# Attention in single-bank tiles: float32 projections in quarter tiles, steps by halves of the heads, squares of the prologue summed by TensorE

## The chip, the cores and the metric

One Trainium2 chip, one of its cores. The metric is device time in microseconds; the median of three runs is given where there are several. Engines: TensorE (PE; its weight loads are PEld), VectorE (DVE), ScalarE (ACT), GpSimd (POOL) and SyncE (SP), which here only issues transfers.

## What is computed

Attention with random features for 4 batches of 8 heads, 576 tokens, head width 64 and 128 features, and behind it two feed-forward layers, the first with one expert per token out of 8.

```python
def phi(x):                                   # x = q or k, scaled by 64 ** -0.25
    proj = np.einsum('bhsd,md->bhsm', x, omega)
    h = proj - np.sum(x * x, axis=-1, keepdims=True) / 2.0
    return np.exp(h - np.max(h, axis=-1, keepdims=True)) / np.sqrt(m)
kv = np.einsum('bhsm,bhsd->bhmd', k_p, v)
num = np.einsum('bhsm,bhmd->bhsd', q_p, kv)
den = np.einsum('bhsm,bhm->bhs', q_p, np.sum(k_p, axis=2))[..., None] + 1e-06
x = (num / den)                               # then by tokens: 2304 x 512
expert_idx = np.argmax(x @ w_gate, axis=1)    # one expert: relu(x @ w1) @ w2, times its probability
out = np.maximum(x @ w_in, 0.0) ** 2 @ w_out
```

All of it is float32.

## The kernel before, in words

The 2304 tokens are 18 tiles of 128; a batch of 576 tokens is four and a half tiles, so tiles 4 and 13 belong to two batches (`pieces`). The order of every instruction is written out by hand: each engine works through its own queue in the order of the program, and SP's and POOL's queues issue the transfers.

For each K tile and each Q tile the kernel loads the tile twice, with the features down the partitions (`load`, L164) and with the tokens down the partitions (`load_rows`, L184). The first copy is split into a high part (`colsplit`, ScalarE, L223) and a rest (`colrest`, L234, POOL, or VectorE for the first seven K tiles). `proj` (L238) multiplies both with the two parts of omega: 12 matmuls of 256 columns into two PSUM banks of four heads each. The second copy is squared on POOL (`squares`, L201) and summed on VectorE (`sums`, L208). `most` (L262) takes the maxima of both banks on VectorE, `shift` (L268, L270) makes the bias of eight heads, and `expo` (L282) runs eight exponentials of 128 columns on ScalarE.

A K tile then goes into `kv_part` (L297): 16 float32 matmuls in half tiles (128 rows, 64 columns) that add the tile to its batch's product, in banks `w0` and `w1` until the batch ends. `kv_close` copies it out; `kvg_turn` (L320) and `kvg` (L329) append its product with the gate weights. A Q tile goes through `t_step` (L348, eight transposes into the pair of banks `t`; half is copied out by ScalarE, half by VectorE in `t_rest`), `n_step` (L369, 16 float32 matmuls in half tiles of 73 columns, then denominator, reciprocal and division for all heads on VectorE, L377 to L381) and `x_step` (L391, four transposes, one copy to `xT` on ScalarE and one store of `xT` to device memory from SP).

`attention` (L453) has a prologue for K tiles 0 to 4, 13 steps s that each take K tile s+5 and Q tile s, and steps 13 to 17 that take Q tiles alone. A Q tile is projected in step s, exponentiated in step s+1, transposed and multiplied in step s+2, and its x transposed in step s+3. The last two tiles' transposes and numerators stand behind the loop in `main_path`, between the first layers of the first two expert steps. The function `beside` puts the loads and splits of the first batch's expert weights into the steps from 8 on; the expert is chosen by `gating` and `counting` of the first batch in steps 7 and 8. Behind the attention the expert steps run, a batch's half and an eighth of the hidden width at a time, with the other loads and splits at steps that `plan` lists.

PSUM has eight banks: three `pj`, one `x`, the pair `t` and `w0`, `w1`.

Of the kernel before, what the change touches and what calls it, by code (L numbers as in the profile page):

```python
# [15 lines left out]
P = 128  # L16
B, H, S, D = 4, 8, 576, 64
M = 128
# [71 lines left out]
class Kern:  # L90
# [30 lines left out]
    def bank(self, tag, name):  # L121
        return self.ps.tile([P, 512], F32, tag=tag, name=name, bufs=3 if tag == "pj" else 1)

    def banks(self, name):
        return self.ps.tile([P, 2, 512], F32, tag="t", name=name, bufs=1)

    def setup_attn(self):
# [9 lines left out]
        self.hl, self.three = {}, {}  # L137
# [6 lines left out]
        self.womh = self.qpool.tile([P, 2 * M], F32R, name="womh")  # L144
        self.woml = self.qpool.tile([P, 2 * M], F32R, name="woml")
        nc.vector.tensor_copy(self.womh, w)
        nc.vector.tensor_tensor(self.woml, w, self.womh.bitcast(F32), ALU.subtract)
# [14 lines left out]
    def load(self, tag, t):  # L162

        if t >= NT:  # L164
            return
        pool = self.kpool if tag == "kp" else self.qpool
        x = pool.tile([P, DM], F32, tag=tag + "c", name=f"{tag}c{t}", bufs=3 if tag == "kp" else 2)
        self.nc.sync.dma_start(out=x, in_=self.a["kk" if tag == "kp" else "qq"][t, :, 0, :])
        self.cols[tag, t] = x

    def load_v(self, t):
        if t >= NT:
            return
        if len(pieces(t)) == 2:
            self.vin[t] = self.halves
            for i in range(2):
                rows = slice(i * 64, (i + 1) * 64)
                self.nc.sync.dma_start(out=self.halves[i][rows], in_=self.a["vv"][t, rows])
            return
        v = self.kpool.tile([P, H, VW], F32, tag="vin", name=f"vin{t}", bufs=5)  # L180
        self.vin[t] = [v]
        self.nc.sync.dma_start(out=v, in_=self.a["vv"][t])

    def load_rows(self, tag, t):  # L184
        if t >= NT:
            return
        if tag == "kp" and t < 8:
            if t % 2 == 0:
                self.pair = self.stage(f"kpr{t}")
            x = self.pair[:, t % 2 * DM : (t % 2 + 1) * DM]  # L190
        else:
            pool = self.kpool if tag == "kp" else self.qpool
            x = pool.tile([P, DM], F32, tag=tag + "r", name=f"{tag}r{t}", bufs=2)
# [3 lines left out]
    def squares(self, tag, t):  # L197
# [3 lines left out]
        self.nc.gpsimd.tensor_tensor(x, x, x, ALU.mult)  # L201

    def sums(self, tag, t):
        if t >= NT:
            return
        sq = self.rows.pop((tag, t))
        ssq = self.qpool.tile([P, H, 1], F32, tag="ssq", name=f"ssq_{tag}{t}", bufs=3)
        self.nc.vector.tensor_reduce(ssq, sq.rearrange("p (h d) -> p h d", h=H), axis=AX.X, op=ALU.add)  # L208
        three = self.three[tag, t] = self.qpool.tile([P, H, 3], F32, tag="three", name=f"three_{tag}{t}", bufs=5)
        self.nc.gpsimd.tensor_scalar(three[:, :, 1:2], ssq, -0.5 * SCALE * SCALE, None, op0=ALU.mult)  # L210
        if tag == "qp" or t > 5:
            self.load_rows(tag, t + 2)
        if tag == "qp" and t < 13 or tag == "kp" and t > 4:
            self.squares(tag, t + 1)

    def colsplit(self, tag, t):
        if t >= NT:
            return
        nc = self.nc
        pool = self.kpool if tag == "kp" else self.qpool  # L220
        x = self.cols.pop((tag, t))
        hi = pool.tile([P, DM], F32R, tag=tag + "h", name=f"{tag}h{t}", bufs=2)
        nc.scalar.copy(hi, x)  # L223
        self.hl[tag, t] = x, hi

    def colrest(self, tag, t):
        if t >= NT:
            return
        nc = self.nc
        pool = self.kpool if tag == "kp" else self.qpool  # L230
        x, hi = self.hl[tag, t]
        lo = pool.tile([P, DM], F32R, tag=tag + "l", name=f"{tag}l{t}", bufs=2)
        eng = nc.vector if tag == "kp" and t < 7 else nc.gpsimd
        eng.tensor_tensor(lo, x, hi.bitcast(F32), ALU.subtract)  # L234
        self.hl[tag, t] = hi, lo
        self.load(tag, t + (3 if tag == "kp" else 2))

    def proj(self, tag, t):  # L238

        nc = self.nc  # L240
        xh, xl = self.hl.pop((tag, t))
        if tag == "kp" and t in (2, 5):
            ps = [self.bank("pj", f"pj_{tag}{t}"), self.bank("x", f"pj_{tag}{t}_1")]
        elif tag == "kp" and t in (1, 4, 6):
            both = self.banks(f"pj_{tag}{t}")
            ps = [both[:, i, :] for i in range(2)]
        else:
            ps = [self.bank("pj", f"pj_{tag}{t}_{i}") for i in range(2)]
        self.pj[tag, t] = ps
        for c in range(H // 2):  # L250
            out = ps[c // 2][:, c % 2 * 2 * M : (c % 2 + 1) * 2 * M]
            s = slice(c * P, (c + 1) * P)
            nc.tensor.matmul(out, xh[:, s], self.womh, start=(c % 2 == 0), stop=False, skip_group_check=True)
            nc.tensor.matmul(out, xh[:, s], self.woml, start=False, stop=False, skip_group_check=True)
            nc.tensor.matmul(out, xl[:, s], self.womh, start=False, stop=(c % 2 == 1), skip_group_check=True)

    def most(self, tag, t):

        three = self.three[tag, t]
        for i, ps in enumerate(self.pj[tag, t]):  # L260
            out = three[:, 4 * i : 4 * i + 4, 0:1]
            self.nc.vector.tensor_reduce(out, ps.rearrange("p (h m) -> p h m", h=4), axis=AX.X, op=ALU.max)  # L262

    def shift(self, tag, t):

        nc = self.nc
        three = self.three.pop((tag, t))
        nc.vector.tensor_reduce(three[:, :, 2:3], three[:, :, 0:2], axis=AX.X, op=ALU.add, negate=True)  # L268
        bias = self.qpool.tile([P, H], F32, tag="bias", name=f"bias_{tag}{t}", bufs=3)
        nc.vector.tensor_reduce(bias, three[:, :, 1:3], axis=AX.X, op=ALU.add)  # L270
        self.bias[tag, t] = bias

    def expo(self, tag, t):

        nc = self.nc
        ps, bias = self.pj.pop((tag, t)), self.bias.pop((tag, t))
        if tag == "kp":
            y = self.kp[t] = self.kpool.tile([P, H, M], F32, tag=tag, name=f"kp{t}", bufs=3)
        else:
            y = self.qp[t] = self.qpool.tile([P, H, M], F32, tag=tag, name=f"qp{t}", bufs=2)  # L280
        for h in range(H):
            nc.scalar.activation(y[:, h, :], ps[h // 4][:, h % 4 * M : (h % 4 + 1) * M], AF.Exp, bias=bias[:, h : h + 1])  # L282
# [4 lines left out]
    def kv_part(self, b, t, i):  # L287
# [4 lines left out]
        if t == tiles[0]:  # L292
            self.kv_ps[b, i] = self.bank(f"w{i}", f"kv_ps{b}_{i}")
        part = [bb for bb, lo, hi in pieces(t)].index(b)
        for j in range(4):
            for a in range(0, M, 64):
# [4 lines left out]
                    start=(t == tiles[0] and j == 0),  # L301
# [4 lines left out]
    def kv_close(self, b):  # L306
        kv = self.kv[b] = self.qpool.tile([P, 2, 4, XW], F32, tag="kv", name=f"kv{b}", bufs=2)
        self.kvn = self.qpool.tile([P, 2, 4, D], F32, tag="kvn", name=f"kvn{b}", bufs=1)
        for i in range(2):
            ps = self.kv_ps[b, i][:, : 4 * VW].rearrange("p (h w) -> p h w", w=VW)  # L310
            self.nc.vector.tensor_copy(kv[:, i, :, 0:VW], ps)
            self.nc.scalar.copy(self.kvn[:, i], kv[:, i, :, 0:D])

    def kvg_turn(self, b):
# [3 lines left out]
        ps = self.bank("x", f"kvT_ps{b}")  # L318
# [5 lines left out]
    def kvg(self, b):  # L324

        nc = self.nc
        ps = self.bank("x", f"kvg_ps{b}")
# [10 lines left out]
    def t_step(self, t, apart=False):  # L338
        nc = self.nc
        qp = self.qp.pop(t)  # L340
        out = self.qpool.tile([P, 2, 512], F32, tag="qpT", name=f"qpT{t}", bufs=2)
        if apart:
            ps = [self.bank(f"w{i}", f"t_ps{t}_{i}") for i in range(2)]
        else:
            both = self.banks(f"t_ps{t}")
            ps = [both[:, i, :] for i in range(2)]
        for h in range(H):
            nc.tensor.transpose(ps[h // 4][:, h % 4 * P : (h % 4 + 1) * P], qp[:, h, :], self.ident)  # L348
        nc.scalar.copy(out[:, 1, :], ps[1])
        self.qpT[t] = out, ps[0]  # L350

    def t_rest(self, t):
        out, ps = self.qpT[t]
        self.nc.vector.tensor_copy(out[:, 0, :], ps)
        self.qpT[t] = out

    def n_step(self, t):

        nc = self.nc
        qpT = self.qpT.pop(t)  # L360
        x = self.qpool.tile([P, 2, 4, D], F32, tag="xr", name=f"xr{t}", bufs=2)
        lg = self.qpool.tile([P, 2, 4, E], F32, tag="lgh", name=f"lgh{t}", bufs=2)
        rd = self.qpool.tile([P, 2, 4, 1], F32, tag="rd", name=f"rd{t}", bufs=2)
        ps = self.banks(f"n_ps{t}")
        for i in range(2):
            for j in range(4):
                for a in range(0, P, 64):
                    b = next(b for b, lo, hi in pieces(t) if lo <= a < hi)
                    nc.tensor.matmul(  # L369
                        ps[a : a + 64, i, j * XW : (j + 1) * XW],  # L370
                        qpT[:, i, j * P + a : j * P + a + 64],
                        self.kv[b][:, i, j],
                        start=True,
                        stop=True,
                    )
        pv = ps[:, :, : 4 * XW].rearrange("p a (h w) -> p a h w", h=4)
        nc.vector.tensor_scalar(rd, pv[:, :, :, D : D + 1], 1e-6 * M, None, op0=ALU.add)  # L377
        nc.vector.reciprocal(rd, rd)
        nc.vector.tensor_tensor(x, pv[:, :, :, 0:D], rd.to_broadcast([P, 2, 4, D]), ALU.mult)
# [934 lines left out]
```

## Time and profile before

| what | us |
|---|---|
| median of 3 runs | 743.47 (743.17 to 747.55) |
| the profiled execution, device time | 748.41 |
| its span, first to last instruction | 746.9 |
| attention, to the last tile's first transpose | 153.14 |

The profile is of one execution. Its times count from the first instruction. A timeline row gives start, length, engine, line, operation, output and inputs, shape and count; rows of one kind that follow each other are merged. An engine's row says in brackets how long the engine stood idle before it and what ended that.

### The profile page before, as it was taken

What the parts mean: (1) busy time and instruction counts of PE and PEld (TensorE: products, weight loads), DVE (VectorE), ACT (ScalarE), POOL (GpSimd) and SP (SyncE); (2) the same over time, 40 slices, a digit from 0 to 9 for tenths busy, and PEclk for the clock granted to TensorE, in tenths of its full rate; (3) what the DMA queues carried; (4) which work ended last, traced back from release to release, by engine and by line L of the source; (5) the groups of instructions that cost most, each with busy time, mean ns of one, the idle gap of its engine ahead of it and who ended that gap; (6) DMA issues with size and microseconds to landing.
All of it is one profiled execution on the core that took longest, in us unless ns stands there. A gap on an engine that the chain in (4) does not pass through costs nothing.

```text
span 746.9 us, 16913 instructions
## 1 busy us (share of the span) xinstructions
PE 721.7 (97%) x6408; PEld 702.8 (94%) x6408; DVE 560.9 (75%) x1199; ACT 421.0 (56%) x1025; POOL 225.4 (30%) x298
## 2 busy tenths in 40 slices
PE   8899999999999999999999999999999989999996
PEld 7788888898999998999999999999999979999996
DVE  6888987877777667855665769687855898888892
ACT  5888888854455445544664546555742465554551
POOL 4756678811000014263731124144221200000000
PEclk9999999999999999999999999999999999999999
DMA  8757665735767677622043456466766374444421
GB/s 286 250 173 211 210 208 157 220 114 175 243 219 249 227 224 266 210 93 64 29 144 133 171 175 233 179 214 216 266 235 210 115 238 137 140 141 138 134 94 32
DMA packets 74536, 133.86 MB, mean 179 GB/s; under 512 B 8496, under 2 KB 36544, under 8 KB 74448
## 3 DMA queue, kind: packets, MB, share of 16 engines
q1 hardware_dynamic: 62192, 89.76, 36.7%
q0 software_dynamic: 12256, 42.95, 17.7%
q8 instruction: 52, 0.85, 0.5%
q14 instruction: 36, 0.29, 0.1%
HBM read 92.36 MB, written 40.32 MB: 178 GB/s over the span
## 4 chain that ended last, share of the span: by engine, by line
PE 68%; DVE 11%; DMA 8%; ACT 5%; issue 4%; POOL 1%; SPq 0%; ACTq 0%; DVEq 0%; POOLq 0%
PE y L1079 6%; PE y L1077 6%; PE y L1078 6%; PE X L963 4%; PE X L964 4%; PE X L965 4%; PE h L769 4%; PE h L768 4%; PE h L770 4%; PE y L797 3%; PE y L798 3%; PE y L796 3%; PE Z L963 2%; PE Z L964 2%; DMA xT<-wscr 2%
## 5 line engine op out<-in xcount | busy, mean ns | idle before, releaser
L780 ACT ACTIVATE hh<-h 128x288 fp32r<-128x288 f32 x64 | 26.3, 411 | 83.1 <-PE h L770 82.6
L939 ACT COPY xT<-X 128x288 f32<-128x288 f32 x96 | 37.0, 399 | 39.7 <-PE X L965 39.1
L1033 ACT CAST hc<-xT 128x384 fp32r<-128x384 f32 (+1 forms) x76 | 39.2, 563 | 29.7 <-DVE xT L63 18.3
L628 POOL DMA_DIRECT2D we<-we x32 | 17.8, 556 | 112.8 <-DVE hl L781 53.3
L282 ACT ACTIVATE kp<-pj_kp,bias_kp 128x128 f32<-128x128 f32 x144 | 39.3, 397 | 18.1 <-DVE bias_kp L270 15.0
L781 DVE SCALAR_TENSOR_TENSOR hl<-h,hh 128x288 fp32r<-128x288 f32 x64 | 29.0, 453 | 22.9 <-ACT hh L780 22.4
L1079 PE MATMUL y<-wB,hc 128*128 128x256 f32 x152 | 43.4, 286 | 0.6 <-DVE hc L1035 0.6
L1077 PE MATMUL y<-wB,hc 128*128 128x256 f32 x152 | 43.1, 283 | 0.0
L1078 PE MATMUL y<-wB,hc 128*128 128x256 f32 x152 | 43.0, 283 | 0.0
L1035 DVE TENSOR_TENSOR hc<-xT,hc 128x384 fp32r<-128x384 f32 (+1 forms) x76 | 42.2, 618 | 0.0
L282 ACT ACTIVATE qp<-pj_qp,bias_qp 128x128 f32<-128x128 f32 x144 | 39.5, 405 | 2.9 <-DVE rd L377 2.0
L769 PE MATMUL h<-xl,wA 128*128 128x288 f32 x128 | 38.2, 298 | 1.9 <-DVE xl L757 1.9
L732 DVE TENSOR_SCALAR narrow<-narrow 128x512 f32<-128x512 f32 x32 | 15.7, 490 | 31.8 <-ACT narrow L731 31.6
L942 DVE SCALAR_TENSOR_TENSOR xT<-xT 128x288 f32<-128x288 f32 (+1 forms) x64 | 39.3, 650 | 0.0
L797 PE MATMUL y<-hl,wA 128*128 128x288 f32 x128 | 38.0, 297 | 1.3 <-DVE hl L781 1.3
L768 PE MATMUL h<-xh,wA 128*128 128x288 f32 x128 | 38.3, 300 | 0.3 <-ACT xh L755 0.3
L963 PE MATMUL X<-wA,w 128*128 128x288 f32 x128 | 38.0, 297 | 0.5 <-ACT xT L805 0.5
L797 PE MATMUL y<-hl,wB 128*128 128x288 f32 x128 | 37.8, 295 | 0.3 <-DVE hl L781 0.3
L796 PE MATMUL y<-hh,wA 128*128 128x288 f32 x128 | 37.9, 296 | 0.0
L769 PE MATMUL h<-xl,wB 128*128 128x288 f32 x128 | 37.9, 296 | 0.0
L963 PE MATMUL X<-wB,w 128*128 128x288 f32 x128 | 37.9, 296 | 0.0
L768 PE MATMUL h<-xh,wB 128*128 128x288 f32 x128 | 37.8, 296 | 0.0
(247 smaller groups left out, 3001.5 us busy)
## 6 DMA issues: line engine op xcount, KB each, us to landing
hscr<-xT SPq DMA_DIRECT2D x32, 576.0 KB, 3.8
we<-we POOLq DMA_DIRECT2D x32, 512.0 KB, 5.5
xT<-hscr SPq DMA_DIRECT2D x64, 256.0 KB, 4.5
xT<-wscr POOLq DMA_DIRECT2D x48, 256.0 KB, 4.1
wd<-wf SPq DMA_DIRECT2D x22, 512.0 KB, 5.4
wscr<-narrow SPq DMA_DIRECT2D x22, 256.0 KB, 3.0
wd<-wf POOLq DMA_DIRECT2D x10, 512.0 KB, 4.3
kpc<-kk SPq DMA_DIRECT2D x18, 256.0 KB, 3.8
```

The costliest lines, as they stand in the source:

```text
L282: nc.scalar.activation(y[:, h, :], ps[h // 4][:, h % 4 * M : (h % 4 + 1) * M], AF.Exp, bias=bias[:, h : h + 1])
L768: nc.tensor.matmul(ps, w1, xh, start=(c == 0), stop=False)
L769: nc.tensor.matmul(ps, w1, xl, start=False, stop=False)
L796: nc.tensor.matmul(out, w1, hh, start=(f == 0), stop=False)
L797: nc.tensor.matmul(out, w1, hl, start=False, stop=False)
L942: nc.vector.scalar_tensor_tensor(v, v, 0.0, v, op0=ALU.max, op1=ALU.mult)
L963: nc.tensor.matmul(ps, w1, xh[:, r, c], start=(start and c == 0), stop=False, skip_group_check=True)
L964: nc.tensor.matmul(ps, w1, xl[:, r, c], start=False, stop=False, skip_group_check=True)
L1035: nc.vector.tensor_tensor(hc[q].at(1, a, b), raw[:, q, a + 1 : b + 1], hc[q].at(0, a, b).bitcast(F32), ALU.subtract)
L1077: nc.tensor.matmul(ps, h1, w1, start=first, stop=False, skip_group_check=True)
L1078: nc.tensor.matmul(ps, h1, w2, start=False, stop=False, skip_group_check=True)
L1079: nc.tensor.matmul(ps, h2, w1, start=False, stop=last, skip_group_check=True)
```

## The change

The split into high part and rest goes. `proj` multiplies the float32 tile itself, one head at a time, in quarter tiles (64 rows, 64 columns, 128 moving columns): 16 matmuls, where the even heads go to one bank and the odd heads to the other. Every step function works by halves, each with a single-bank tile, and the banks are named `k0`, `k1` (K projections), `q0`, `q1` (Q projections), `t0`, `t1` (transposes, numerators, x, counts) and `w0`, `w1` (kv, kvg).

For K tiles 0 to 4 the rows are not loaded: POOL squares the feature tile and TensorE sums the squares with four float32 matmuls against two columns that hold -0.5 times the squared scale, into free columns of the kv banks. For the other tiles POOL also adds the two halves of the squares, so that VectorE sums 32 columns a head instead of 64.

The numerators' division is cut in two, the order within a step is new, a Q tile is exponentiated in the step in which it is projected and transposed in the next, the gate products of a tile are kept and summed later, and the first batch's choice of an expert is spread over the steps 6 to 9 (`aside`). The loop of Q tiles runs to step 18. x is stored per batch (`x_store`) at the expert steps 2, 6, 10 and 14 instead of per tile.

The core of the diff:

```diff
     def sums(self, tag, t):
-        self.nc.vector.tensor_reduce(ssq, sq.rearrange("p (h d) -> p h d", h=H), axis=AX.X, op=ALU.add)
+        self.nc.vector.tensor_reduce(ssq, sq, axis=AX.X, op=ALU.add)
...
+    def colsums(self, t):
+        sq = self.sqc.pop(t)
+        w = t % 2
+        if t < 2:
+            self.kv_ps[0, w] = self.bank(f"w{w}", f"kv_ps0_{w}")
+        ps = self.kv_ps[0, w][:, 4 * VW + t * H : 4 * VW + (t + 1) * H]
+        for c in range(KC):
+            self.nc.tensor.matmul(ps[:, 2 * c : 2 * c + 2], sq[:, c * P : (c + 1) * P], self.half, start=(t < 2 and c == 0), stop=True, skip_group_check=True)
...
+    def proj(self, tag, t, banks):
+        x = self.cols.pop((tag, t))
+        ps = self.pj[tag, t] = [self.bank(f"{banks}{i}", f"pj_{tag}{t}_{i}") for i in range(2)]
+        for c in range(H // 2):
+            for a in range(0, P, 64):
+                for r in range(2):
+                    rows = slice(r * D, (r + 1) * D)
+                    nc.tensor.matmul(
+                        ps[r][a : a + 64, c * M : (c + 1) * M],
+                        x[rows, c * P + a : c * P + a + 64],
+                        self.wom[rows, r * M : (r + 1) * M],
...
         for s in range(13):
             k = s + 5
+            b = {1: 0, 5: 1, 10: 2}.get(s)
+            if s > 0:
+                self.proj("qp", s, "q")
+            if b is not None:
+                self.kvg_turn(b)
+            self.x_step(s - 2)
+            self.n_lg(s - 2, 1)
+            both("qp", s)
+            self.shift("qp", s)
+            if s > 0:
+                self.sums("kp", k)
+            self.shifted("qp", s)
+            if s > 0:
+                self.proj("kp", k, "k")
+            self.sums("qp", s + 1)
+            self.expo("qp", s, 0)
+            for i, c in ((1, nc.vector.tensor_copy), (0, nc.vector.tensor_copy if s < 3 else nc.scalar.copy)):
+                self.t_step(s - 1, i, "t", c)
+            self.t_copy(s - 1, 1)
+            self.t_copy(s - 1, 0)
+            if b is not None:
+                self.kvg(b)
+            self.expo("qp", s, 1)
+            self.most("kp", k, 0)
+            if b is None:
+                kv(s + 4)
+            self.most("kp", k, 1)
+            self.shift("kp", k)
...
+            self.load_v(k + 1)
+            self.n_step(s - 1, 0)
+            self.n_step(s - 1, 1)
+            self.n_den(s - 1, 0)
+            if s > 0:
+                self.shifted("kp", k)
+            self.n_rec(s - 1, 0)
+            self.n_den(s - 1, 1)
+            self.n_out(s - 1, 0)
+            self.n_lg(s - 1, 0)
+            self.n_rec(s - 1, 1)
+            expo("kp", k)
+            self.n_out(s - 1, 1)
...
+        for b in range(B):
+            at(2 + 4 * b, self.x_store, b)
```

## Rows read from the trace of the kernel before

**Rows 1.** The page's first part: busy time and share of TensorE.
```profile
PE 721.7 (97%) x6408; PEld 702.8 (94%) x6408; DVE 560.9 (75%) x1199; ACT 421.0 (56%) x1025; POOL 225.4 (30%) x298
```

**Rows 2.** Stretches of 10 us: busy time of each engine, clock, DMA share, GB/s.
```profile
60.00:70.00 10.00, 9.98 (x150) 9.09 (x148) 9.28 (x22) 9.21 (x29) 6.82 (x9) 1.00 0.71 221
...
200.00:210.00 10.00, 10.00 (x78) 10.00 (x77) 8.56 (x17) 5.24 (x11) 0.77 (x2) 1.00 0.67 230
```

**Rows 3.** Timeline of TensorE: transposes of Q tiles 0, 3, 12 and 17.
```profile
35.10 1.85 PE L348 MATMUL t_ps<-ident,qp 128*128 128x128 f32 x8 [2.23 <-ACT kp L282]
...
59.76 1.03 PE L348 MATMUL t_ps<-ident,qp 128*128 128x128 f32 x8
...
129.63 1.09 PE L348 MATMUL t_ps<-ident,qp 128*128 128x128 f32 x8
...
153.14 1.09 PE L348 MATMUL t_ps<-ident,qp 128*128 128x128 f32 x8
```

**Rows 4.** Timeline of TensorE in step 6.
```profile
66.85 1.04 PE L348 MATMUL t_ps<-ident,qp 128*128 128x128 f32 x8
67.73 0.60 PE L320 MATMUL kvT_ps<-ident,kvn 128*128 128x128 f32 x4
68.26 1.15 PE L297 MATMUL kv_ps<-vin,kp 128*64 128x65 f32 x32
69.34 1.07 PE L329 MATMUL kvg_ps<-wg,kvT 128*128 128x16 f32 x8
70.25 0.36 PE L253 MATMUL pj_kp<-womh,kph 128*128 128x256 f32 x1
...
71.59 0.28 PE L255 MATMUL pj_kp<-womh,kpl 128*128 128x256 f32 x1
71.79 1.25 PE L369 MATMUL n_ps<-kv,qpT 128*64 128x73 f32 x32
72.97 0.66 PE L391 MATMUL x_ps<-ident,xr 128*128 128x128 f32 x4
73.39 0.37 PE L253 MATMUL pj_qp<-womh,qph 128*128 128x256 f32 x1
```

**Rows 5.** Timeline of VectorE in step 6.
```profile
68.14 0.68 DVE L208 TENSOR_REDUCE ssq_kp<-kpr 128x8 f32<-128x512 f32 x1
...
72.70 0.17 DVE L268 TENSOR_REDUCE three_kp<-three_kp 128x8 f32<-128x16 f32 x1
```

**Rows 6.** Timeline of ScalarE in step 6.
```profile
68.94 2.19 ACT L282 ACTIVATE qp<-pj_qp,bias_qp 128x128 f32<-128x128 f32 x8
70.95 0.69 ACT L223 CAST kph<-kpc 128x512 fp32r<-128x512 f32 x1
73.17 1.66 ACT L282 ACTIVATE kp<-pj_kp,bias_kp 128x128 f32<-128x128 f32 x6 [1.54 <-DVE bias_kp L270]
```

**Rows 7.** Groups of 0 to 300 us: count, busy us, mean ns, idle before.
```profile
L262 DVE TENSOR_REDUCE three_qp<-pj_qp 128x4 f32<-128x512 f32 x36 | 23.9, 685 | 1.5 <-PE pj_qp L255 0.7
...
L234 POOL TENSOR_TENSOR qpl<-qpc,qph 128x512 fp32r<-128x512 f32 x18 | 23.0, 1279 | 27.7 <-ACT qph L223 27.6
```

**Rows 8.** Short stretches of the numerators: matmuls, then weight loads, in flight.
```profile
71.79:71.80 0.01, 0.01 (x2) 0.01 (x2) 1.00 1.05 410
...
71.91:71.92 0.01, 0.01 (x4) 0.01 (x6) 1.00 4.01 819
```

**Rows 9.** Timeline of the prologue, all engines.
```profile
4.11 0.62 ACT L223 CAST kph<-kpc 128x512 fp32r<-128x512 f32 x1 [1.86 <-DMA kpc<-kk]
...
5.77 0.41 PE L255 MATMUL pj_kp<-womh,kpl 128*128 128x256 f32 x1
5.98 0.41 PE L253 MATMUL pj_kp<-womh,kph 128*128 128x256 f32 x1
...
11.77 2.17 ACT L282 ACTIVATE kp<-pj_kp,bias_kp 128x128 f32<-128x128 f32 x8 [3.22 <-DVE bias_kp L270]
...
30.24 2.23 ACT L282 ACTIVATE qp<-pj_qp,bias_qp 128x128 f32<-128x128 f32 x8
```

More of the change, by code (lines that the diff above doesn't have):

```diff
@@ L227, in colrest, with most @@
+    def most(self, tag, t, r):
         if t >= NT:
             return
-        nc = self.nc
[L230 to L282, printed above, removed]
+        three = self.trio(tag, t).rearrange("p (c r) k -> p r c k", r=2)
@@ L291, in kv_part @@
         tiles = self.tiles_of(b)
-        if t == tiles[0]:
+        if t == tiles[0] and (b, i) not in self.kv_ps:
             self.kv_ps[b, i] = self.bank(f"w{i}", f"kv_ps{b}_{i}")
@@ L300, in kv_part @@
                     self.vin[t][part][:, 4 * i + j, :],
[L301 removed]
+                    start=(t == tiles[0] and j == 0 and b > 0),
                     stop=(t == tiles[-1]),
@@ L352, in t_rest @@
[L352 to L379, printed above, removed]
-        nc.vector.tensor_tensor(lg, pv[:, :, :, VW:], rd.to_broadcast([P, 2, 4, E]), ALU.mult)
-        nc.vector.tensor_reduce(self.lg[:, t, :], lg.rearrange("p a h e -> p e (a h)"), axis=AX.X, op=ALU.add)
-        self.xr[t] = x.rearrange("p a h d -> p (a h d)")
@@ new lines, in t_step, with t_copy @@
+    def t_step(self, t, i, tag, copy):
+        if not 0 <= t < NT:
+            return
+        qp = self.qp[t]
+        ps = self.bank(f"{tag}{i}", f"t_ps{t}_{i}")
+        for j in range(4):
+            self.nc.tensor.transpose(ps[:, j * P : (j + 1) * P], qp[:, 4 * i + j, :], self.ident)
+        out = self.qpT[t, i] = self.qpool.tile([P, 512], F32, tag=f"qpT{i}", name=f"qpT{t}_{i}", bufs=2)
+        self.tps[t, i] = lambda: copy(out, ps)
+    def t_copy(self, t, i):
+        if 0 <= t < NT:
+            self.tps.pop((t, i))()
@@ new lines, in n_step @@
+    def n_step(self, t, i):
+        nc = self.nc
+        if not 0 <= t < NT:
+            return
+        qpT = self.qpT.pop((t, i))
+        ps = self.bank(f"t{i}", f"n_ps{t}_{i}")
+        for j in range(4):
+            for a in range(0, P, 64):
+                b = next(b for b, lo, hi in pieces(t) if lo <= a < hi)
+                nc.tensor.matmul(
+                    ps[a : a + 64, j * XW : (j + 1) * XW],
+                    qpT[:, j * P + a : j * P + a + 64],
+                    self.kv[b][:, i, j],
+                    start=True,
+                    stop=True,
+                    skip_group_check=True,
+                )
+        self.nps[t, i] = ps[:, : 4 * XW].rearrange("p (h w) -> p h w", h=4)
```

415 lines of the change are left out of this document (241 added, 174 removed).

## The prediction

> **What bounds the kernel now.** I read the page's engine shares first: TensorE counts as busy for 97% of the span [rows 1], but that is a mean over two different stages. The stretches of 10 us tell them apart [rows 2]: from 200 us on TensorE alone is full (10.00 of 10, VectorE 8.56, ScalarE 5.24), while at 60 to 70 us TensorE, VectorE and ScalarE are all at 9 to 10 of 10. The change touches only this first stage, which ends with the transposes of the last tile at 153.14 us [rows 3]. What comes behind is bound by TensorE and is untouched, apart from one set of stores. So the gain is how much earlier that last transpose starts.
>
> Inside the stage I read one step on each engine. On TensorE the step runs from one `t_ps` to the next; its pieces in order are transposes 0.88, turn of kv 0.53, kv 1.08, kvg 0.9, K projection 1.54, numerators 1.18, x 0.42 (I use 0.5), Q projection 1.4 without its wait for a bank [rows 4]. I take pieces from start to start, since busy times of single matmuls overlap: the first and the last of the 12 matmuls of the K projection lie 1.34 apart, 0.12 a matmul, so 12 are about 1.4. On VectorE a sum of squares over 512 columns takes 0.68 and a small reduction of the bias 0.17 [rows 5]. On ScalarE eight exponentials take 2.01 (68.94 to 70.95) and a split copy 0.69, and ScalarE stood 1.54 us waiting for VectorE's bias [rows 6]. A maximum over 512 columns costs VectorE 0.685, and POOL's subtraction for the low part 1.28 [rows 7]. No engine is the bound by itself: the step with no kvg from tile 3 (59.76) to tile 4 (66.85) is 7.1 us, where TensorE's pieces sum to about 6.5. From the first `t_ps` at 35.10 to that of tile 12 at 129.63 are 12 steps, 7.88 each on average; from there to tile 17 at 153.14 are 23.5 us [rows 3].
>
> **The change part by part.** (1) *Projection.* Gone per tile: 12 matmuls, about 1.4 us, the split copy on ScalarE (0.69, some 0.6 of it not overlapped) and the subtraction on POOL (1.28) or, for the first K tiles, on VectorE. New: 16 float32 matmuls of 64 rows by 64 columns with 128 moving columns. No row of before has this form. The nearest is the numerators: 16 float32 matmuls in half tiles (x32 records, two passes each), 73 columns, 1.18 us, so 37 ns a record; kv, 65 columns, 1.08 us, so 34 ns [rows 4]. The eight columns more cost 3.1 ns, 0.39 per column, and 7 to 8 ns a record is fixed. Alone, a pass of 128 columns would be 128 x 0.39 x 2 = 100 ns. Four at once: 25 + 8 = 33 ns x 32 = 1.05 us. Two at once: 50 + 7 = 57 x 32 = 1.8 us. One after another: 107 to 113 x 32 = 3.5 us. I take four at once, 1.05, because the half tiles really start together: within the first 10 ns of the numerators two matmuls are in flight, and a third and fourth only at 71.91 [rows 8]. If tiles of a column half run beside each other, quarters that write different banks should too.
>
> What the rows show here is that pairs start together. The Trainium skill (TensorE: Matmul & The Clock Gate, part 3 on packing small matmuls) says that matmuls start and end in strict program order. If the two passes of one matmul stand behind each other in that order and share a tile, the next matmul can't start before the second pass, and only two of four tiles work: 1.8 us. By that rule the second matmul of rows 8 should not have started within 10 ns, so the trace speaks against that reading for half tiles; no run here shows it for quarters.
>
> The change of tile form has a price too: from the last K projection start (71.59 [rows 4]) to the numerators it is 0.20 instead of 0.12, some 0.08 a switch; the new step has five switches for four, 0.1 us, inside my rounding. The same skill (TensorEngine Tiling (Array Packing), Key Properties) says that a change of mode drains the engine; 0.08 us is what that drain is worth here.
>
> (2) *The other engines.* Per step VectorE had four maxima 2.7, two sums of squares 1.4, a copy of 512 columns 0.7, four bias reductions 0.7 and the division's five instructions about 1.5 (an estimate by width from the same rows): 7.0. The sums now read 256 columns instead of 512, 0.35 to 0.4 each (-0.6); the gate sum of some 0.3 leaves the steps; the division in two halves costs three small instructions more, +0.3 to 0.5: 6.4 to 6.5. ScalarE had exponentials 4.0, splits 1.2, two copies 1.0 to 1.2 = 6.3, and has 5.1. POOL loses two subtractions of 1.28 and gains two additions of 256 columns, half as long: -1.3. These are sums of busy times, of which neighbours overlap by 0.05 to 0.1 each.
>
> (3) *The step.* TensorE's new sum is 2 x 1.05 + 0.5 + 0.88 + 1.1 + 1.18 = 5.8 (K and Q projection 2.1, x, transposes, kv, numerators). But the K banks are single: the K projection of step s starts when ScalarE has ended the K exponentials of step s-1. From there: projection 1.05, transposes 0.88, kv 1.1, first numerators 0.6, then VectorE's denominator and the bias behind it 0.4 with handovers, then eight exponentials 2.0, plus 0.3 for handovers = 6.3 us. That chain closes on itself, so it is the step; the Q branch fits beside it (its bias comes about 1.3 us after the K exponentials end, its exponentials and the copy of the transposes are done before the K bias). I add 0.3 for collisions: 6.6. Three steps with kvg cost 0.8 more each. Twelve steps: 12 x 6.6 + 2.4 = 81.6 for 94.5: **12.9 us**. Lower bound TensorE's own 5.8 to 6.0 (another 7 us), upper bound a good step of today, 7.1, with 0.1 for the switch: 7.2.
>
> (4) *Prologue.* The first exponentials wait at 11.77 for a bias that waits for row squares loaded behind other transfers, though the first K tile was there at 4.11 [rows 9]. Now the squares come from that tile: POOL up to 1.28 for one 512-column instruction, four float32 matmuls against two columns. Their price is near that of kvg, x8 records in 0.9 us [rows 4], doubled at the start, where matmuls lie 0.21 apart instead of 0.12 [rows 9]. First projection 1.8 at that pace, maxima 1.3, biases 0.5: first exponentials at about 8.6. Then the tiles follow at 2.3 to 3.4 (TensorE: 0.9 + 1.05 + 1.1 = 3.05 while ScalarE needs 2.0): the fifth ends near 21, the first Q tile follows at once instead of at 30.24 [rows 9], and since the Q tile is now transposed one step after its projection (before: two), the first `t_ps` comes after Q tile 0 (23.1), K tile 5 (25.2) and a K projection, at 26.3 for 35.10: **8.8 us**. Bounds 5 (that slow pace at every tile) to 11.
>
> (5) *Tail.* Per tile TensorE loses 0.35 and ScalarE 0.5, and one more step is run, but it replaces the code for two tiles that stood behind the loop. TensorE 3.6, ScalarE 3.7 with expert casts, VectorE 4.2; I take 4.2 a step: 5 x 4.2 + 1.6 for the first hidden layer (12 matmuls of 288 columns, an estimate from 0.12 for 256) = 22.7 for 23.5: **0.8 us**. Bounds -3 to +4.
>
> (6) *Stores.* The 20 stores of x (one per piece of a tile) leave SP's queue in the steps, where they cover nothing, and come back as four of 1.18 MB at the expert steps 2, 6, 10 and 14, ahead of loads of expert and output weights. At the 230 GB/s of that time [rows 2] each takes 5.1 us. TensorE is fed from buffers there, so I cost it at **-1 us**; without that cover up to -3.
>
> Sum: 12.9 + 8.8 + 0.8 - 1 = 21.5. The profiled execution took 748.41 (746.9 and 1.5 around it), so its like would be 726.9. It lay 4.9 above the median of 743.47; from the median 21.5 less is **722**.
>
> **The rivals.** *Two quarters at once* (1.8 us a projection): TensorE's step becomes 7.3, with collisions 7.5, the prologue gives 5.3, the tail loses 2.2: 743.5 - (2.1 + 5.3 - 2.2 - 1) = 739. For it: nothing here shows four. Against it: rows 8. *The order by hand is too tight*: the quarters run at 1.05, but each step waits as today's (7.2) since one late bias holds VectorE's queue with the maxima of the other tile behind it, and no second K bank absorbs it: 12 x 7.2 + 2.4 = 88.8, 7.2 us less gain, 729. For it: the waits of ScalarE on VectorE in rows 6; against it: all three engines have less to do. *Quarter tiles one after another* is the slower one: a projection 3.5 us, TensorE 10.7 a step, 12 steps 131 (37 lost), the tail 12 lost, the prologue nothing won: 743.5 + 50 = 794. It decides from about 1.95 us a projection (24 projections in 12 steps give back 21.5 at 0.9 more). Against it: half tiles are not serial. That the stores starve the experts is a matter of 3 us and inside the range.
>
> **How the numbers follow.** Forecast 0.62, two at once 0.17, tight order 0.13, serial 0.08. Range: low end 712, from steps of 6.0 (-7) and the prologue's better bound (-2) and a little; high end 739, the first rival; about a tenth is left above and under a tenth below. A measurement of this kernel can tell about 1% (7.4 us) from no change. Faster by over 1% (under 736): 0.60 + 0.05 + 0.12 = 0.77. Within: 0.02 + 0.11 + 0.01 = 0.14. Slower: 0.01 + 0.08 = 0.09.
>
> **What would show it.** Projection pieces of about 1.05 us from start to start of the next piece, first exponentials near 8.6, the first `t_ps` near 26, tile 12's near 108, tile 17's near 131; no POOL subtraction left; TensorE's idle time before the K projection put down to the K exponentials. Wrong, if a projection takes 1.8 or more, if ScalarE's waits for the biases grow instead of shrinking, or if TensorE shows new gaps in the expert steps after the stores.

## The result and the profile after

| | before | changed |
|---|---|---|
| median of 18 runs each | 744.77 us (741.05 to 747.83) | 737.66 us (732.85 to 743.49) |
| ratio, 95% interval | | 0.9911 [0.9885, 0.9936] |
| the profiled execution | 748.41, span 746.9 | 734.66, span 733.1 |

The change is faster by 7.1 us. 21.5 were forecast. The two profiled executions lie 13.8 apart, which is more than the medians show: the one before lay above its median and the one after below. So the steps of the forecast are read from the traces, stage by stage, and the sum is set against the medians.

First the page's shares, then two stretches of 10 us (busy time of TensorE, its weight loads, VectorE, ScalarE and POOL; granted clock; DMA share; GB/s), of the changed kernel. They answer to [rows 1, 2].

```profile
PE 707.2 (96%) x7168; PEld 684.2 (93%) x7168; DVE 543.5 (74%) x1251; ACT 402.7 (55%) x985; POOL 209.3 (29%) x299
```

```profile
60.00:70.00 10.00, 9.96 (x234) 8.92 (x236) 8.59 (x30) 7.66 (x28) 6.13 (x10) 1.00 0.66 205
200.00:210.00 10.00, 9.46 (x71) 9.22 (x70) 4.11 (x7) 3.03 (x7) 0.24 (x1) 1.00 0.99 389
```

In the steps ScalarE's busy time fell from 9.21 to 7.66 of 10 us and VectorE's from 9.28 to 8.59. At 200 us, in the expert steps, TensorE now has gaps (9.46 for 10.00) while DMA is full (0.99, 389 GB/s).

TensorE's timeline of the changed kernel: the transposes of Q tiles 0, 4, 6, 12 and 17 (for those of [rows 3]), and between them projections of steps 6 and 7.

```profile
30.60 1.09 PE L351 MATMUL t_ps<-ident,qp 128*128 128x128 f32 x8
...
59.10 1.09 PE L351 MATMUL t_ps<-ident,qp 128*128 128x128 f32 x8
...
63.42 1.10 PE L247 MATMUL pj_qp<-wom,qpc 64*64 64x128 f32 x32
64.45 0.66 PE L409 MATMUL x_ps<-ident,xr 128*128 128x128 f32 x4
...
71.68 1.10 PE L247 MATMUL pj_kp<-wom,kpc 64*64 64x128 f32 x30 [0.15 <-ACT kp L288]
72.71 1.09 PE L351 MATMUL t_ps<-ident,qp 128*128 128x128 f32 x8
...
113.87 1.06 PE L351 MATMUL t_ps<-ident,qp 128*128 128x128 f32 x8 [0.39 <-DVE lgh L398]
...
141.40 1.09 PE L351 MATMUL t_ps<-ident,qp 128*128 128x128 f32 x8 [0.83 <-ACT qp L288]
```

A projection takes 1.03 us (63.42 to 64.45). The K projection at 71.68 waits 0.15 us for the K exponentials. These rows give the account:

| step of the forecast | forecast | measured |
|---|---|---|
| prologue, to the first `t_ps` (35.10, now 30.60) | -8.8 | -4.5 |
| 12 steps (94.5, now 113.87 - 30.60 = 83.3) | -12.9 | -11.2 |
| tail, tile 12 to 17 (23.5, now 27.5) | -0.8 | **+4.0** |
| stores | +1 | +1.5 (by the experiment below) |

That is 10.2 for 21.5. Two terms are missed by 4 to 5 us each, and the tail has the wrong sign.

### The profile page after: what moved, and what is told of

The parts are those of the page before. It is cut to its first block, busy times and chain, and to the rows that moved or that the text cites. A ratio compares the mean times of both kernels' runs of the same rounds, so it can differ in the third digit from the quotient of the medians.

```text
span 733.1 us, 18313 instructions
## 1 busy us (share of the span) xinstructions
PE 707.2 (96%) x7168; PEld 684.2 (93%) x7168; DVE 543.5 (74%) x1251; ACT 402.7 (55%) x985; POOL 209.3 (29%) x299
## 5 line engine op out<-in xcount | busy, mean ns | idle before, releaser
L884 DVE SCALAR_TENSOR_TENSOR hl<-h,hh 128x288 fp32r<-128x288 f32 x64 | 29.0, 453 | 22.0 <-ACT hh L883 21.5
L1048 DVE SCALAR_TENSOR_TENSOR xT<-xT 128x288 f32<-128x288 f32 (+1 forms) x64 | 38.3, 636 | 0.0
L871 PE MATMUL h<-xh,wA 128*128 128x288 f32 x128 | 38.3, 299 | 0.0
```

The costliest lines, as they stand in the source:

```text
L871: nc.tensor.matmul(ps, w1, xh, start=(c == 0), stop=False)
L1048: nc.vector.scalar_tensor_tensor(v, v, 0.0, v, op0=ALU.max, op1=ALU.mult)
```

## The experiments

Each of the twelve kernels is the changed one, or the one before, with the edits shown (after_again has none). Ratios are to the kernel before. Most edits move the time by 1 to 3 us, of which a ratio tells little; where that is so, the verdict rests on the starts of `t_ps` in one profiled execution each: the twelve steps took 82.9 to 83.7 us in each profile of a kernel that doesn't change them, as long as the clock stayed at full (84.7 in the last one, best).

**Is it four quarters at once?** The loop order of the projection, so that two quarters of one row half follow each other:

```diff
-        for c in range(H // 2):
-            for a in range(0, P, 64):
-                for r in range(2):
+        for r in range(2):
+            for c in range(H // 2):
+                for a in range(0, P, 64):
```

> The changed kernel with the 16 matmuls of a projection in another order: first all for the even heads (rows 0 to 63), then all for the odd ones, so that only two quarters can work at a time. Theory: four quarters at once is what makes 1.04 us; two at once costs 1.7 to 1.9 us a projection, each step loses 0.7 to 1.5 us, and the kernel is slower by 12 to 20 us than the changed one, ratio to before 1.007 to 1.02. Rival: the projection isn't on the path of the step, and the time stays within 4 us of the changed kernel's (ratio under 0.997).

Ratio 1.006 [1.0023, 1.0098], some 12 us above the changed kernel. TensorE's timeline of this kernel:

```profile
68.69 1.59 PE L247 MATMUL pj_qp<-wom,qpc 64*64 64x128 f32 x32
70.22 0.66 PE L409 MATMUL x_ps<-ident,xr 128*128 128x128 f32 x4
```

The same 16 matmuls take 1.53 us (68.69 to 70.22) instead of 1.03. How many records start together can be read from the trace in stretches of a hundredth of a microsecond (TensorE's busy time and records of the projection in flight; clock; DMA share; GB/s), first of the changed kernel, then of this one:

```profile
63.42:63.44 0.02, 0.02 (x4) 1.00 0.53 208
63.44:63.57 0.13, 0.13 (x4) 1.00 0.54 160
```

```profile
68.69:68.71 0.02, 0.01 (x2) 1.00 0.00 0
68.71:68.85 0.14, 0.14 (x2) 1.00 0.46 164
```

In the changed kernel four records start within 20 ns, and the next four follow about every 109 ns. Here they start in pairs at the same pace, except in the middle, from 0.50 to 0.89 us behind the first start, where the pairs of the second row half already run beside those of the first. So four run at once in the changed kernel, and the overlap of all four is worth more than the whole gain of the change. The two quarters of a row half also write one bank; which of the two keeps them to pairs is not separated.

**The quarter tiles alone**, in the kernel before with its own banks and order (even heads to one bank, odd heads to the other, no split, feature tiles loaded one tile further ahead):

```diff
-            out = ps[c // 2][:, c % 2 * 2 * M : (c % 2 + 1) * 2 * M]
...
+                    nc.tensor.matmul(
+                        ps[r][a : a + 64, c * M : (c + 1) * M],
```

> The kernel before with the projection alone changed: 16 float32 matmuls in quarter tiles, no split of the tile, everything else (order, banks, rows for the squares, x per tile) as before. Theory: the split's copies and subtractions and 0.4 us of TensorE a projection were most of the gain in the steps; the steps fall from 7.9 to 7.0 to 7.3 us and the time by 8 to 12 us, as much as or more than the whole change gives, since the slower tail isn't in it: ratio 0.984 to 0.990. Rival: without the new order and the single banks the steps wait as before, and the gain is under 3 us (ratio over 0.996).

My theory fell: 1.0387 [1.0339, 1.0434], 29 us slower. TensorE's timeline of this kernel:

```profile
85.00 0.43 PE L235 MATMUL pj_qp<-wom,qpc 64*64 64x128 f32 x2
87.18 1.10 PE L235 MATMUL pj_qp<-wom,qpc 64*64 64x128 f32 x30 [1.75 <-ACT kp L270]
...
90.31 0.43 PE L235 MATMUL pj_kp<-wom,kpc 64*64 64x128 f32 x2
92.15 1.10 PE L235 MATMUL pj_kp<-wom,kpc 64*64 64x128 f32 x30 [1.41 <-ACT qp L270]
```

Of each projection the first head (2 records) starts, and the other 30 records wait for the exponentials of the tile before: odd and even heads write both banks from the first pair on. The kernel before fills its first bank with six matmuls while ScalarE still reads the second. To see whether that coupling is the cause, and not the quarter tiles, I gave it to the kernel before, which keeps its 12 matmuls:

```diff
-        for c in range(H // 2):
+        for c in (0, 2, 1, 3):
...
-        for h in range(H):
+        for h in (0, 4, 1, 5, 2, 6, 3, 7):
```

> The kernel before with its own 12 matmuls a projection, but in an order that writes both banks by turns (heads 0-1, 4-5, 2-3, 6-7), and exponentials that read both banks by turns. Nothing else is changed and no instruction added. Theory (quarter tiles alone lost 29 us because they need both banks at once and so wait for the exponentials of the whole tile before): the steps grow to 9-11 us as in proj_alone, 15 to 30 us slower than before, with projections that wait for exponentials and a lower clock in places. Rival (the loss lay in the quarter tiles themselves or in their loads): within 1% of before.

1.0285 [1.0214, 1.0357], some 20 us slower with the same instructions in another order. Its TensorE:

```profile
61.61 0.28 PE L255 MATMUL pj_qp<-womh,qpl 128*128 128x256 f32 x1
63.30 0.38 PE L253 MATMUL pj_qp<-womh,qph 128*128 128x256 f32 x1 [1.41 <-ACT kp L282]
...
66.85 0.28 PE L255 MATMUL pj_kp<-womh,kpl 128*128 128x256 f32 x1
68.14 0.39 PE L253 MATMUL pj_kp<-womh,kph 128*128 128x256 f32 x1 [1.02 <-ACT qp L282]
```

After three matmuls it waits as the quarter tiles did, and the steps grow to 9.5 us on average (35.0 to 149.3 for the twelve). The clock, which I had expected lower in places, was full in these steps, so it isn't what costs. The other 9 us of proj_alone are not taken apart; its clock was at the lower level for 20.5 us between 34 and 131 us. Quarter tiles paid only together with the new banks (`k`, `q`, `t`, `w`), which let a projection start while the other tensor's banks are still read; that the banks are what made the difference is argued, since no run has the new banks with the old matmuls.

**The tail.** ScalarE copies x out of the bank `t0`, which the numerators want next (4.7 us of TensorE's waiting in six times). The x transposes of the tail go to `w0` and `w1`:

```diff
-            self.x_step(s - 2)
+            self.x_step(s - 2, f"w{s % 2}" if s > 13 else "t0")
```

> The changed kernel, but from step 14 on the transposes of x go to the free banks w0 and w1 instead of t0, which the numerators of the same step need next. Theory: the tail lost its time because the numerators wait for ScalarE's copy of x out of t0 (seven waits of 0.67 to 1.10 us before the numerators, 5.1 us in all); with another bank the six waits from step 14 on shrink to the 0 to 0.3 us that the copy of the transposes still asks for, the stretch from the transposes of tile 12 to those of tile 17 falls from 27.5 to 23.5 to 24.5 us, and the kernel takes 3 to 4 us less: ratio to before near 0.986. Rival: the tail is bound by ScalarE's exponentials and copies; then the numerators start earlier but the transposes of the next tile wait for the exponentials instead, the stretch stays at 26.5 us or more, and the ratio stays at 0.990.

The rival was right. Five of the six waits for x went (the one of step 13 lies ahead of the edit), and `t_ps` 12 to 17 still took 27.6 us (27.5): TensorE now waits for the Q exponentials instead, 2.3 us in three times. This is the wait that ends last, and ScalarE's timeline of the changed kernel shows what it stands on:

```profile
136.72 0.59 ACT L353 COPY qpT<-t_ps 128x512 f32<-128x512 f32 x1 [0.33 <-PE t_ps L351]
138.26 0.41 ACT L883 ACTIVATE hh<-h 128x288 fp32r<-128x288 f32 x1 [0.95 <-PE h L873]
138.69 0.58 ACT L413 COPY xT<-x_ps 128x512 f32<-128x512 f32 x1
139.17 2.18 ACT L288 ACTIVATE qp<-pj_qp,bias_qp 128x128 f32<-128x128 f32 x8
141.18 1.10 ACT L722 CAST wA<-we 128x1024 fp32r<-128x1024 f32 x1
```

The transposes start at 135.53, the copy follows, then ScalarE stands 0.95 us for the first hidden layer, copies x, and only then comes to the exponentials on which the next transposes (141.40) wait. In the kernel before, a Q tile was transposed a whole step after its exponentials; now it is the next thing, and every copy that stands ahead of them in ScalarE's queue lies on the path. So, with the x banks of tail_bank, the exponentials were moved up:

```diff
             self.t_copy(s - 1, 0)
+            if s > 13:
+                expo("qp", s)
```

> The changed kernel with x in the w banks from step 14 on (as in tail_bank), and from step 14 on the Q exponentials stand on ScalarE right behind the copy of the transposes, ahead of the first layer's activation and the copy of x. Theory (the tail is bound by ScalarE's order: copy, wait of 0.95 us for the first layer, copy of x, exponentials, weight cast, and only then the next transposes): t_ps 12 to t_ps 17 falls from 27.5 to 24.5-25.5 us, the wait of t_ps for the exponentials (0.83 at tile 17) goes. Rival (the tail is bound by VectorE, whose bias comes about 2 us behind t_ps anyway): 27-28 us, unchanged, and the copies of the transposes come later instead.

The theory held: 116.0 to 141.3 is 25.3 us, and the wait is gone from the transposes of tile 17 (ratio 0.984 [0.9782, 0.9898]). TensorE's and ScalarE's timelines of this kernel:

```profile
136.90 1.10 PE L351 MATMUL t_ps<-ident,qp 128*128 128x128 f32 x8
...
141.29 1.09 PE L351 MATMUL t_ps<-ident,qp 128*128 128x128 f32 x8
```

```profile
139.06 2.18 ACT L288 ACTIVATE qp<-pj_qp,bias_qp 128x128 f32<-128x128 f32 x8 [0.33 <-DVE bias_qp L275]
141.08 0.46 ACT L886 ACTIVATE hh<-h 128x288 fp32r<-128x288 f32 x1
```

Not quite half of the tail's miss of 4.8 is this order (2.2). VectorE's bias is what is late next. As much lies in the first step of the tail, which took 6.65 us in this kernel as in the changed one, for 4.2 forecast. TensorE's timeline of the changed kernel:

```profile
114.86 1.15 PE L303 MATMUL kv_ps<-vin,kp 128*64 128x65 f32 x32
...
117.81 1.25 PE L369 MATMUL n_ps<-kv,qpT 128*64 128x73 f32 x32 [1.10 <-ACT xT L413]
...
120.52 1.04 PE L351 MATMUL t_ps<-ident,qp 128*128 128x128 f32 x8
```

The last K tile's kv (1.19 us from start to start) now stands behind tile 12's transposes, where the kernel before had it ahead of them; it, the turn of kv behind it (0.49) and the kvg of the next step (0.91) are in no term of the forecast's tail. Which of this and of the 1.10 us for the copy of x is on the path no run takes apart.

**The stores.** x is stored per tile again, four large stores go:

```diff
+            nc.sync.dma_start(out=self.xscr[:, :, t * P + lo : t * P + hi], in_=here)
...
-            at(2 + 4 * b, self.x_store, b)
```

> The changed kernel with x stored per tile during the attention again, as before, and no stores of 1.18 MB in the expert steps. Theory: the four large stores delay loads of expert weights and cost TensorE 1 to 2 us between 170 and 220 us (there its busy time is 9.34, 9.46 and 8.91 of 10 us in three stretches); without them these gaps close and the time falls by 1 to 2 us, nothing is lost in the attention: ratio near 0.989. Rival: the gaps have another cause (the first loads of the second batch's expert wait for its choice), and the time stays as it is or rises by the transfers in the steps.

From the first matmul of the experts' second layer to the 600th matmul of the experts it is 81.3 us for 82.8 with the large stores (80.9 before), start to start, and the attention is unchanged (first `t_ps` 30.3, tile 17 141.2). That is 1.5 us, by these two traces; the ratio of 0.9871 [0.9829, 0.9914] can't tell it. Over all profiles with the clock at full there it is 80.9 to 81.3 with stores per tile and 81.7 to 83.3 with the large ones. The stretch that showed gaps above, in this kernel:

```profile
200.00:210.00 10.00, 10.00 (x77) 10.00 (x76) 5.29 (x11) 5.18 (x10) 0.49 (x1) 1.00 0.74 248
```

**The prologue.** ScalarE's timeline of the changed kernel, for that of [rows 9]:

```profile
8.17 1.28 ACT L288 ACT_TABLE_LOAD   x1 [8.17 <-DVE bias_kp L275]
9.47 6.30 ACT L288 ACTIVATE kp<-pj_kp,bias_kp 128x128 f32<-128x128 f32 x24
19.00 2.17 ACT L288 ACTIVATE kp<-pj_kp,bias_kp 128x128 f32<-128x128 f32 x8 [3.24 <-PE kv_ps L303]
22.10 2.17 ACT L288 ACTIVATE kp<-pj_kp,bias_kp 128x128 f32<-128x128 f32 x8 [0.93 <-PE kv_ps L303]
24.46 2.17 ACT L288 ACTIVATE qp<-pj_qp,bias_qp 128x128 f32<-128x128 f32 x8 [0.18 <-DVE bias_qp L275]
27.00 2.17 ACT L288 ACTIVATE kp<-pj_kp,bias_kp 128x128 f32<-128x128 f32 x8 [0.37 <-DVE bias_kp L275]
```

The first bias is there at 8.17, but the load of the activation table stands behind the same wait, since nothing else of ScalarE's comes before the exponentials now; in the kernel before ScalarE loaded it at 0.96, ahead of its split. (The Trainium skill, ScalarE: Activation LUTs, What ACT_TABLE_LOAD costs, has 1283 ns for one; the trace agrees with its 1.28.) Then the fourth tile waits 3.24 us for kv to give back one of three buffers. Two stretches of TensorE of this kernel tell why kv was late:

```profile
5.00:10.00 5.00, 5.00 (x111) 1.00 0.77 260
10.00:20.00 10.00, 9.95 (x136) 0.66 0.88 285
```

From 11.6 the granted clock was at the lower of its two levels (1.2 instead of 2.4 GHz) for 6.8 us, after 5 us in which TensorE was never idle. In the kernel of stores_back, with the same prologue and as busy a TensorE, the clock stayed at 1.00 from 10 to 20 us, the fourth tile's exponentials came at 16.7 instead of 19.0, and yet the first `t_ps` came at 30.3: there K tile 5 waited 3.02 us for its bias:

```profile
27.09 2.17 ACT L288 ACTIVATE kp<-pj_kp,bias_kp 128x128 f32<-128x128 f32 x8 [3.02 <-DVE bias_kp L275]
```

The edits take these causes one by one. First, a dummy exponential of two columns ahead of all else on ScalarE:

```diff
+        early = self.qpool.tile([P, 2], F32, name="early")
+        self.nc.scalar.activation(early, self.half, AF.Exp)
```

> The changed kernel with one dummy exponential of two columns ahead of everything on ScalarE, so that the load of the activation table (1.28 us) no longer stands between the first bias and the first exponential. Both theories: first exponentials 8.2-8.9 instead of 9.5. Theory A (the prologue is a chain of projections, exponentials and buffers): everything behind moves too, first t_ps 29.0-29.5 instead of 30.3-30.6. Theory B (the rows of the later tiles, loaded behind other transfers, set the end of the prologue): first t_ps stays within 0.4 of 30.5 and the time doesn't move.

Theory A: exponentials at 8.11, first `t_ps` at 29.45, with as long a stretch of low clock as in the changed kernel. Second, VectorE's sum of Q tile 1 moved behind K tile 5:

```diff
-            self.sums("qp", s + 1)
+            if s > 0:
+                self.sums("qp", s + 1)
...
             expo("kp", k)
+            if s == 0:
+                self.sums("qp", 1)
```

> The changed kernel where in step 0 the sum of squares of Q tile 1 stands on VectorE behind the bias of K tile 5 instead of ahead of its maxima. Theory B (VectorE stands for the rows of Q tile 1 with K tile 5's maxima queued behind it: 2.6 us in the run with the stores per tile): K tile 5's exponentials start at 24-25.5 instead of 27.0, first t_ps 27.5-29. Theory A (the chain of projections, exponentials and buffers): K tile 5's exponentials stay at 26.5-27 and the first t_ps at 30-30.6.

Theory B: exponentials of K tile 5 at 25.33, first `t_ps` at 28.8, here with the clock at full. Both fit, each by one execution: with the low clock the chain is late, and without it the queue order is. POOL's timeline of sums_late shows the rest of it:

```profile
22.59 1.04 POOL L195 TENSOR_TENSOR qpr<-qpr 128x512 f32<-128x512 f32 x1 [4.03 <-DMA qpr<-qq]
23.71 0.73 POOL L197 TENSOR_TENSOR qpr<-qpr 128x256 f32<-128x256 f32 x1
24.52 0.24 POOL L211 TENSOR_SCALAR three_kp<-ssq_kp 128x8 f32<-128x8 f32 x1
```

POOL too stands 4.03 us for the rows of Q tile 1 with K tile 5's bias term behind them. Both edits together, with POOL's order mended and kv moved ahead of the projections:

```diff
+            if t > 1:
+                kv(t - 2)
             if t < 3:
                 self.colsquares(t + 2)
...
-                self.sums("kp", 5)
+                self.sums("kp", 5, False)
+                self.squares("qp", 1)
+                self.squares("kp", 6)
```

> The changed kernel with four edits in the prologue: the activation table loaded at the start (table_early), the sum of squares of Q tile 1 behind K tile 5 on VectorE (sums_late), POOL's squares of Q tile 1 and K tile 6 behind its bias term of K tile 5, and each kv ahead of the projection two tiles on. Theory (K tile 5 stands in VectorE's and in POOL's queue for rows that belong to a later tile; without that its exponentials follow those of Q tile 0): exponentials of K tile 5 at 22.5-24.5 instead of 27.0, first t_ps 26-28 instead of 30.5, some 3 us less time. Rival (the transfers themselves, of K tile 5 and of the V tiles, are as late): exponentials of K tile 5 at 25 or later, first t_ps 28.5-29.5.

By its numbers this is the rival's: K tile 5 at 25.25 and first `t_ps` at 28.6, ratio 0.9888 [0.9837, 0.9938]. The changed kernel ran beside it:

> The changed kernel as it is, once more, beside the others on the same chip. Both theories: ratio 0.988 to 0.993, first t_ps 30.3-31, t_ps 12 to 17 27.5.

0.9888 [0.9847, 0.9929], first `t_ps` at 33.5 after 10.2 us at the lower clock, tail 27.5. So in time the four edits show no difference. In the trace K tile 5 no longer waits for anything:

```profile
17.99 2.18 ACT L291 ACTIVATE kp<-pj_kp,bias_kp 128x128 f32<-128x128 f32 x8 [2.60 <-DVE bias_kp L278]
21.09 2.18 ACT L291 ACTIVATE kp<-pj_kp,bias_kp 128x128 f32<-128x128 f32 x8 [0.92 <-DVE bias_kp L278]
23.24 2.18 ACT L291 ACTIVATE qp<-pj_qp,bias_qp 128x128 f32<-128x128 f32 x8
25.25 2.23 ACT L291 ACTIVATE kp<-pj_kp,bias_kp 128x128 f32<-128x128 f32 x8
```

It follows Q tile 0 directly; what was late is K tile 3's bias (2.60), which stood for sums of squares on TensorE, behind a projection and a kv in a stretch of 3.4 us at the lower clock. Transfers, which the rival named, hold nothing on this chain.

Last, the part of the change that sets the first exponentials free was undone: rows of K tiles 0 to 4 are loaded and squared on POOL and summed on VectorE.

```diff
-        for t in range(3):
+        for t in range(2):
             self.load("kp", t)
+            self.load_rows("kp", t)
...
-        self.colsquares(0)
-        self.colsquares(1)
+        self.squares("kp", 0)
...
-            self.colsum("kp", t + 1)
+            if t < 4:
+                self.sums("kp", t + 1)
```

> The changed kernel without the squares summed by TensorE: rows of K tiles 0 to 4 are loaded, squared and added on POOL and summed on VectorE, as for the other tiles. Theory (this part of the change set the first exponentials free, as forecast): first exponentials 11-13 instead of 9.5, first t_ps 31.5-34 instead of 30.5. Rival (rows for later tiles set the end of the prologue anyway): first exponentials as late, but the first t_ps within 0.5 of 30.5.

The theory held only in part. The first exponentials came at 10.46, 1.0 us later and not 1.5 to 3.5, but the third K tile waited 6.27 us and the fifth 4.16, and the first `t_ps` came at 38.3: ratio 1.0009 [0.9977, 1.0041], all of the gain gone. The bias of the third stands behind rows that POOL waits 5.84 us for:

```profile
12.82 2.17 ACT L288 ACTIVATE kp<-pj_kp,bias_kp 128x128 f32<-128x128 f32 x8 [0.19 <-DVE bias_kp L275]
21.27 2.17 ACT L288 ACTIVATE kp<-pj_kp,bias_kp 128x128 f32<-128x128 f32 x8 [6.27 <-DVE bias_kp L275]
```

13.6 us at the lower clock in this prologue are part of that, and not in this execution alone: the ten runs have a mean clock of 0.982 to 0.988. What the squares on TensorE are worth at equal clock is therefore not shown.

**All findings together**: prologue_all, tail_order and stores_back.

> The four edits of prologue_all, the tail of tail_order and x stored per tile as in stores_back, all on the changed kernel. If the three findings add up: first t_ps 26-28, t_ps 12 to 17 about 25.3, the expert steps 1.4 us shorter, together 6 to 8 us less than the changed kernel, ratio to before 0.976-0.982. If they don't (what is won ahead is waited for at the first expert weights): 0.984-0.988.

732.96 us beside 739.12 of the changed kernel, ratio 0.9818 [0.9779, 0.9857]: faster than both kernels, at the upper edge of what was expected. The tail (25.3) and the expert steps (81.0 for 82.8) are there; the prologue isn't in the profiled execution (first `t_ps` 31.7, with 6.8 us at the lower clock).

## Why the prediction was right and wrong

*Projection, step 1: right.* 1.03 us for 1.05, and by the half-tile rows I had rightly held against the strict reading of program order. (The Trainium skill, TensorE: Matmul & The Clock Gate, part 3, has matmuls start and end in strict order; that is no limit to two at once here, since four records start within 20 ns.) The 100 ns that I had worked out for a pass alone are 109 in the trace, from one group of four to the next.

*The step, 3: nearly, and in part by luck.* The closed chain over the K exponentials is there (0.15 at 71.68 in the timeline above, 1.3 us in six times), and the twelve steps took 83.3 for 81.6. But the eight with a K tile and without kvg took 6.4 to 7.6, 6.9 on average, for 6.6, and the three with kvg 7.2 to 8.1 for 7.4; the last, which has no K tile, took 4.6 where I had counted 6.6, and hid it. ScalarE's waits for biases, which should have shrunk, went from 10.5 to 9.7 us in the twelve. And the 94.5 for the kernel before were read with a piece of lower clock in them (below): at equal clock the steps gave about 9.6 for 12.9.

*Prologue, step 4: failed by 4.3.* In the kernel with the clock at full (stores_back) the fifth K tile ended at 22.0 (forecast: near 21), Q tile 0 at 24.1 (23.1), but K tile 5 at 29.3 (25.2). The doubled pace at the start, which I had counted, did not show: in the changed kernel the first projection took 1.04 us and its sums of squares 0.98. So about 1 us is the table load, which I had not placed, and 3 us is the sentence "the first `t_ps` comes after Q tile 0, K tile 5 and a K projection": it follows TensorE and ScalarE and not what is queued ahead of K tile 5's bias on VectorE and POOL, the rows of a later tile. In the profiled execution K tile 5 waited only 0.37 us for its bias; there the chain ahead of it was late, with 6.8 us at the lower clock.

*Tail, step 5: failed by 4.8.* I took 4.2 us a step as the fullest engine's sum, and left out kv, turn and kvg, 2.6 us of TensorE. In its last two steps, 5.1 and 5.9 us, the tail is a chain through ScalarE's queue: copy, wait for the first layer, copy of x, exponentials, next transposes. tail_order gave back 2.2 of the 4.8; 2.45 lie in the first step. The two tiles less of pipelining, which I had counted as a gain, made the exponentials urgent.

*Stores, step 6: right*, 1.5 for 1.

*From 10.2 to 7.1.* The profile of the kernel before has a stretch at the lower clock in its first step; the first transposes took 1.85 us where later ones take 1.03 [rows 3]. Its step, with the columns of [rows 2], and its kvg:

```profile
35.10:45.10 10.00, 9.59 (x108) 8.77 (x109) 5.23 (x13) 6.24 (x21) 5.23 (x7) 0.83 0.55 177
```

```profile
39.24 1.07 PE L329 MATMUL kvg_ps<-wg,kvT 128*128 128x16 f32 x8
```

TensorE's timeline of before_coupled, with the same instructions in the same place and the clock at full:

```profile
35.00 1.09 PE L348 MATMUL t_ps<-ident,qp 128*128 128x128 f32 x8 [1.50 <-ACT kp L282]
...
37.55 1.07 PE L329 MATMUL kvg_ps<-wg,kvT 128*128 128x16 f32 x8
```

From the first transposes to kvg it is 4.14 us in the one and 2.55 in the other. TensorE was busy for 9.59 of the 10 us of this step, so what it lost was hardly made up: about 1.6 us of the 11.2 are the clock's and not the change's, and 8.6 are left. By the runs whose clock is recorded, the changed kernel's mean granted clock was 0.9940 (24 runs) and the kernel before's 0.9965 (32 runs); within either a thousandth goes with 0.6 to 0.75 us. That is 1.5 to 1.9 us given back and leaves 6.7 to 7.1, beside 7.1 measured. This sum is an estimate, and its closeness may be chance: behind the attention two profiles of the changed kernel, both at full clock there until the last few us, took 591.7 and 596.8 us.

Direction and range held; the amount was a third of the forecast. That 737.7 lies in the range is luck, since its upper end was the price of two quarters at once, which didn't come. Why the same prologue gets the lower clock in one execution and not in another stays open. The rival of the tight order named VectorE's queue and steps of 7.2: the steps lie between it and the forecast, and what tail_order shows in the tail is another queue, ScalarE's.

## What to carry to other kernels

When a pipeline is made shorter by a step, list for the new consumer everything that stands ahead of its producer in that engine's queue: sums of busy time no longer bound such a stage. Follow the queues of the engines that only prepare (VectorE, POOL) as closely as those that compute, and ask which of their instructions wait for data of a later tile. A faster instruction that needs two buffers at once can be slower than one that takes them in turn: order of banks first, then the form of the matmul.

## What was not expected of the hardware

Float32 matmuls in quarter tiles, 16 of 128 moving columns: 1.03 us with all four quarters in turn, 1.53 when the two of a row half follow each other. That is not the 1.8 that I had worked out for two at once, since in the middle both row halves run together; why the second starts before the first has ended is not shown. The same 12 matmuls and 8 exponentials in another order of banks cost some 20 us over the kernel. In the same prologue the granted clock was at its lower level for 0 us (stores_back), 6.8 (the changed kernel) and 10.2 (after_again).
